# Choosing VectorE's key tiles while the order is planned, instead of from a fixed list, with new pacing constants (attention + MLP on one core)

## The chip, the cores and the metric

The kernel runs on one core of one Trainium2 chip. The metric is device time in microseconds (us). Before the change three runs gave 844.11, 850.04 and 851.01 us, median 850.04. The span is the time from the first to the last instruction of the profiled execution; the granted clock is the share of TensorE's full clock that it was given. TensorE is called PE; the profile calls VectorE DVE, ScalarE ACT and GpSimd POOL.

## The reference, cut to what matters

```python
x = A_x                                    # 1 x 2048 x 512, bf16
xn = layernorm(x)
qkv = (xn @ wqkv)                          # 32 heads of 16
p = softmax(q k^T / 4);  a = (p v) @ wo
h = gelu_tanh(layernorm(x) @ w1 + b1)      # 1792 wide
return x + a + (h @ w2 + b2)
```

With 32 heads of width 16 the costly part is not the products but the exponentials: 32 x 2048 x 2048 of them.

## The kernel before

The work is cut into 32 groups: four heads and 512 queries each. A group has 16 key tiles of 128 keys, and a key tile is four units, one per head. A unit is one 128x512 score matmul into one PSUM bank. Units go one of two ways:

- ScalarE takes units in tiles of two or three PSUM banks and writes `exp` to SBUF.
- VectorE reads the four units of a key tile from PSUM, turning each score by an add and a maximum into the bits of an f16 number (an approximate exponential). It then makes four copies with shifted bits, and PE adds up five weighted products with V, which mends the approximation.

```python
# ScalarE's way (line 1137)
nc.scalar.activation(p_sb[:, s0:s1, :]..., ps[:, b0:b0 + n, :]..., AF.Exp, scale=1.0 / STEP)
# VectorE's way: four reads of PSUM (line 1182), then four shifted copies (line 1205)
nc.vector.tensor_scalar(out=ib[sl][:, j, :], in0=ps[:, pool.bank(key), :],
                        scalar1=LEVEL, scalar2=0.0, op0=ALU.add, op1=ALU.max)
nc.vector.tensor_scalar(out=tb[x % NTB]..., in0=ib[sl]..., scalar1=float(SHIFT[t]),
                        scalar2=None, op0=ALU.add)
```

Nothing is decided on the chip. A planner in the Python code gives every operation a duration and a priority, lists the operations engine by engine, and so fixes the order of the instructions when the kernel is built. For PE it may choose among all candidates that could start within `TOL` of the earliest, and may delay the scores that feed ScalarE by up to `OVER`:

```python
TOL = 0.225
OVER = 0.4
...
end = min(x[0] for x in hot) + self.OVER         # hot: operations that feed ScalarE
cand = [c for c in cand if c[1] in hot or c[0] + c[1].dur + (...) <= end]
...
t, op = min((c for c in cand if c[0] <= first + tol), key=lambda c: (c[1].prio - ..., c[1].seq))
```

How many key tiles of each group VectorE gets stands in a list (111 in all), which fixes ScalarE's stream of tiles before planning starts:

```python
KD = (2, 5, 8, 11, 14)
KD_OF = [(KD if g > 1 else KD2)[:n] for g, n in enumerate((0, 0, 2, 4, 4, 4, 4, 4, 3, ...))]
...
units += [(g, k, j) for g in range(2, NG) for k in range(NT) if k not in KD_OF[g]
          for j in range(HS)]
```

The sums of every group are normalised by a detour: the row sums go by DMA to DRAM and back, are inverted on VectorE, go to DRAM again, and come back spread over 128 partitions (the broadcast, `rlb`). The planner gives the issue of this last DMA 0.5 us and believes that it lands 2.2 us after that, so 2.7 us after the issue begins:

```python
e3 = add("SP", 0.5, lambda: I(nc.sync.dma_start(rlb[:], bcast(rdram[i2]))),
         [e3, last_rlb[0]], pr - 500, lat=2.2)
```

PE also runs matmuls on zeros ("fill"), where the planner expects it to be idle; they are meant to keep its clock up.

## Time and profile before

| | before |
|---|---|
| time, median of 3 | 850.04 us |
| profiled execution | 846.28 us, span 844.5 us, mean granted clock 0.987 |
| ScalarE | 782.0 us busy, 62.5 idle |
| PE | 774.2 us busy, of it 64.2 on fill |
| VectorE | 742.2 us busy |
| ScalarE's waits on scores | 39.8 us in 72 |

How they are read, and the lines themselves, stand in the prediction.

### The profile page before, as it was taken

What the parts mean: (1) busy time and instruction counts of PE and PEld (TensorE: products, weight loads), DVE (VectorE), ACT (ScalarE), POOL (GpSimd) and SP (SyncE); (2) the same over time, 40 slices, a digit from 0 to 9 for tenths busy, and PEclk for the clock granted to TensorE, in tenths of its full rate; (3) what the DMA queues carried; (4) which work ended last, traced back from release to release, by engine and by line L of the source; (5) the groups of instructions that cost most, each with busy time, mean ns of one, the idle gap of its engine ahead of it and who ended that gap; (6) DMA issues with size and microseconds to landing.
All of it is one profiled execution on the core that took longest, in us unless ns stands there. A gap on an engine that the chain in (4) does not pass through costs nothing.

```text
span 844.5 us, 23945 instructions
## 1 busy us (share of the span) xinstructions
PE 774.2 (92%) x10251; PEld 260.6 (31%) x10251; DVE 742.2 (88%) x1281; ACT 782.0 (93%) x681; POOL 55.5 (7%) x163
## 2 busy tenths in 40 slices
PE   6999989999989999998988899999989999998996
PEld 3333333233323332322323233323322333322332
DVE  6867989988999979779899979996699998997987
ACT  3999999999999999999999899998999999998995
POOL 2300000000000000000000000000001000000101
PEclk9999999999999999999999999999999999999998
DMA  5400220000010210000001021000001012101000
GB/s 175 114 2 3 65 59 26 11 15 28 23 31 32 53 37 27 22 21 3 15 22 34 22 52 53 21 14 21 23 16 36 25 28 60 32 10 28 25 10 33
DMA packets 54800, 28.03 MB, mean 33 GB/s; under 512 B 40613, under 2 KB 50598, under 8 KB 54690
## 3 DMA queue, kind: packets, MB, share of 16 engines
q1 hardware_dynamic: 52818, 25.03, 10.8%
q8 instruction: 81, 1.33, 0.7%
q10 hardware_dynamic: 1872, 1.44, 0.6%
q14 instruction: 29, 0.24, 0.1%
HBM read 23.85 MB, written 2.61 MB: 31 GB/s over the span
## 4 chain that ended last, share of the span: by engine, by line
DVE 41%; PE 31%; ACT 12%; issue 8%; DMA 7%; POOL 0%; DVEq 0%; ACTq 0%; SPq 0%
DVE x_sb L1182 16%; ACT p_sb L1137 12%; PE ps L569 12%; DVE tb_x L1205 10%; PE ps L1009 9%; PE ps L991 9%; DMA rlb<-rdram 6%; DVE x_sb L1205 5%; DVE ht L1360 2%; DVE osb L1239 1%; DVE ont L1253 1%; PE ps L1514 1%; DMA rdram<-rc 1%; DVE stats L684 1%; DVE wkv L1393 1%
## 5 line engine op out<-in xcount | busy, mean ns | idle before, releaser
L1137 ACT ACTIVATE p_sb<-ps 128x1024 bf16<-128x1024 f32 (+1 forms) x655 | 741.2, 1247 | 43.7 <-PE ps L991 39.8
L1182 DVE TENSOR_SCALAR x_sb<-ps 128x512 int16<-128x512 f32 x444 | 296.4, 681 | 30.9 <-PE ps L991 30.3
L991 PE MATMUL ps<-qz,kt 32*128 32x512 bf16 x2048 | 280.3, 383 | 39.4 <-ACT p_sb L1137 29.7
L1205 DVE TENSOR_SCALAR tb_x<-x_sb 128x2048 int16<-128x2048 int16 x296 | 198.8, 683 | 2.9 <-PE ps L1009 1.4
L991 PEld LDWEIGHTS <-kt 32*128 32x128 bf16 x2048 | 79.7, 91 | 280.5 <-issue 276.3
L1009 PE MATMUL ps<-p_sb,va 128*32 128x512 bf16 x1604 | 128.6, 386 | 2.4 <-DVE x_sb L1182 2.0
L1009 PE MATMUL ps<-tb_x,vs 128*32 128x512 f16 x1184 | 109.8, 388 | 2.1 <-DVE tb_x L1205 2.0
L1205 DVE TENSOR_SCALAR x_sb<-x_sb 128x2048 int16<-128x2048 int16 x148 | 100.8, 681 | 1.5 <-PE ps L1009 0.7
L1009 PEld LDWEIGHTS <-vs 128*32 128x32 bf16 x1776 | 48.8, 95 | 70.7 <-issue 51.6
L1514 PE MATMUL ps<-ones_bf,zeros_bf 128*32 128x512 bf16 x708 | 64.2, 407 | 4.7 <-issue 3.1
L1009 PEld LDWEIGHTS <-va 128*32 128x32 bf16 x2048 | 40.1, 94 | 83.6 <-issue 79.2
L1009 PE MATMUL ps<-x_sb,vs 128*32 128x512 f16 x592 | 58.9, 386 | 3.9 <-DVE x_sb L1205 3.1
L1260 POOL TENSOR_SCALAR okt<-lc 128x16 f32<-128x16 f32 x31 | 13.7, 442 | 734.3 <-DMA lc<-ldram 734.3
L569 PE MATMUL ps<-yT,w_r 128*32 128x512 bf16 x896 | 58.4, 380 | 3.6 <-DVE x_sb L1182 1.6
L569 PE MATMUL ps<-w_sb,ht 128*32 128x512 bf16 x896 | 60.5, 385 | 0.0
L1009 PE MATMUL ps<-x_sb,va 128*32 128x512 f16 x444 | 44.4, 389 | 3.4 <-DVE osb L1239 2.3
L1360 DVE TENSOR_SCALAR ht<-ps,b_sb 128x512 bf16<-128x512 f32 x56 | 41.7, 744 | 4.8 <-PE ps L569 4.4
L1253 DVE TENSOR_TENSOR ont<-osb,rlb 128x512 bf16<-128x512 f32 x31 | 21.3, 686 | 20.4 <-DMA rlb<-rdram 20.4
L569 PE MATMUL ps<-wo_pad,ont 128*32 128x512 bf16 x512 | 34.6, 384 | 1.1 <-DVE ont L1289 1.1
L569 PEld LDWEIGHTS <-w_r 128*32 128x32 bf16 x896 | 23.5, 96 | 28.1 <-issue 11.7
L569 PEld LDWEIGHTS <-ht 128*32 128x32 bf16 x896 | 21.4, 97 | 24.6 <-issue 9.6
L1514 PEld LDWEIGHTS <-zeros_bf 128*32 128x32 bf16 x708 | 17.2, 99 | 35.7 <-issue 31.7
(92 smaller groups left out, 371.8 us busy)
## 6 DMA issues: line engine op xcount, KB each, us to landing
rlb<-rdram SPq DMA_DIRECT2D x31, 256.0 KB
w_r<-in_B_w_dram SPq DMA_DIRECT2D x56, 128.0 KB
x_r<-in_A_x_dram SPq DMA_DIRECT2D x16, 128.0 KB
w_sb<-in_B_w_dram SPq DMA_DIRECT2D x1, 1792.0 KB
out_dram<-ot SPq DMA_DIRECT2D x12, 128.0 KB
x_sb<-in_A_x_dram SPq DMA_DIRECT2D x2, 512.0 KB
wkv<-in_A_wqkv_dram ACTq DMA_DIRECT2D x1, 512.0 KB
x_sb<-in_A_x_dram ACTq DMA_DIRECT2D x1, 512.0 KB
```

The lines of the kernel that those rows point to most:

```text
L569: I(nc.tensor.matmul(dst[32 * j:32 * j + 32], lhsT=lhsT[:, 32 * j:32 * j + 32], rhs=rhs, start=start, stop=stop, tile_position=(0, 32 * j)))
L684: I(nc.vector.bn_stats(out=stats[:, t, :], in_=x_sb[:, t, :]))
L991: I(nc.tensor.matmul(ps[:, bank, :], lhsT=kt[lo:lo + 32, s // 2, k * P:(k + 1) * P], rhs=qz[lo:lo + 32, (qt * NB + s // 2) % NQB, s % 2, : ...
L1009: I(nc.tensor.matmul(ps[32 * j:32 * j + 32, o_bank[g], :], lhsT=vals[:, h * VS:h * VS + 32], rhs=wts(j), start=st, stop=(pv_left[g] == 0), ...
L1137: I(nc.scalar.activation(p_sb[:, s0:s1, :].rearrange("p a b -> p (a b)"), ps[:, b0:b0 + n, :].rearrange("p a b -> p (a b)"), AF.Exp, scale ...
L1182: I(nc.vector.tensor_scalar(out=ib[sl][:, j, :], in0=ps[:, pool.bank(key), :], scalar1=LEVEL, scalar2=0.0, op0=ALU.add, op1=ALU.max))
L1205: I(nc.vector.tensor_scalar(out=tb[x % NTB].rearrange("p j q -> p (j q)"), in0=ib[sl].rearrange("p j q -> p (j q)"), scalar1=float(SHIFT[t ...
L1239: e0 = add("DVE", dve(QW), lambda: I(nc.vector.tensor_copy(osb[:, i2, :], ps[:, o_bank[g], :])), pvs + before, pr - 1000, rel=(o_done(g),))
L1253: e4 = add("DVE", dve(QW), lambda: I(nc.vector.tensor_tensor(out=ont[:, slot, :], in0=osb[:, i2, :], in1=rlb[:], op=ALU.mult)), [e3] + lis ...
L1260: I(nc.gpsimd.tensor_scalar(out=okt[:, 0, :], in0=lc[:, i2, :], scalar1=L_MIN, scalar2=None, op0=ALU.is_ge))
L1360: I(nc.vector.tensor_scalar(out=ht[:, fc, :], in0=ps[:, misc.bank(key), :], scalar1=b1_sb[:, fc:fc + 1], scalar2=None, op0=ALU.add))
L1514: I(nc.tensor.matmul(ps[32 * j:32 * j + 32, OB if opened is None else o_bank[opened], :], lhsT=zeros_bf[:, 0:32], rhs=ones_bf[:], start=op ...
```

## The change

The intent: let the planner decide which key tiles go to VectorE, at the moment in the plan at which VectorE is nearly through with what it has. The list goes; every group from the third on keeps five spare key tiles, and whichever engine gets there first takes them.

```diff
-    KD_OF = [(KD if g > 1 else KD2)[:n] for g, n in enumerate((0, 0, 2, 4, 4, ...))]
+    left_d = {g: list(KD) if g > 1 else [] for g in range(NG)}
+    left_a = {g: [k for k in range(NT) if k not in KD] if g > 1 else [] for g in range(NG)}
...
+    def next_d():
+        if len(todo) >= OPEN or d_busy[0] >= OUT:          # OPEN 1, OUT 3
+            return
+        g0 = max(stream["g"], 2)
+        for g in (g0, g0 + 1):                             # this group or the next
+            if g >= NG or not left_d[g]:
+                continue
+            if g == stream["g"] and units_left(g) + HS * len(left_d[g]) < (RES if g < NG - 1 else RESL):
+                continue
+            k = left_d[g][0]
+            deps = qk_deps(g, k)
+            if deps is None or not all(o.done for o in deps):   # its K and Q must be projected
+                return
...
+            left_d[g].pop(0)
+            todo.append((g, k, [0, 1, 2, 3]))
+            d_busy[0] += 1
+            build_dve(g, k)
+            return
...
+            k = left_a[g].pop(0) if left_a[g] else left_d[g].pop()    # ScalarE takes what is left
```

With it comes a new set of constants (cut):

```diff
-    TOL = 0.225
+    TOL = 0.075
-    OVER = 0.4
+    OVER = 0.3
-    OUT0, OUT1 = 0.775, 0.4
-    HLO, HHI, DN0, DN1 = 0.09, 0.42, 0.5, 0.12
-    PAIR = 2
-    VX = 0
-    HOT = 4
+    OUT0, OUT1 = 0.475, 0.25
+    HLO, HHI, DN0, DN1 = 0.09, 0.36, 0.5, 0.12
+    PAIR = 1
+    VX = 1
+    KTP, QTP = 70.0, 70.0
+    HOT = 1
-    RATE, QO, PO, AO, DO = 24.25, 55.0, 47.0, 35.0, 32.0
+    RATE, QO, PO, AO, DO = 23.75, 55.0, 39.5, 25.0, 17.0
-            pr = T0 + KG * tq - 4 if b == 0 else ts_(2 * b, tq / 4.0) - 40
+            pr = T0 + KG * tq - 4 if b == 0 else ts_(2 * b, tq / 4.0) - KTP      # projection of K
-        pr = ts_(2 * n) - 50.0
+        pr = ts_(2 * n) - QTP                                                    # projection of Q
```

The `KTP` and `QTP` edits make the projections of K and Q due 70 us ahead of their group, instead of 40 and 50. At the very start, transposes, projections and fill are one 128-column matmul (`mm1`) where four 32-column ones stood.

## The prediction

> **What bounds the kernel now.** I read the page's engine shares first, then its groups, then who ScalarE waited for, then single stretches in order of time.
>
> ```profile
> span 844.5 us, 23945 instructions
> ...
> PE 774.2 (92%) x10251; PEld 260.6 (31%) x10251; DVE 742.2 (88%) x1281; ACT 782.0 (93%) x681; POOL 55.5 (7%) x163
> ...
> L1137 ACT ACTIVATE p_sb<-ps 128x1024 bf16<-128x1024 f32 (+1 forms) x655 | 741.2, 1247 | 43.7 <-PE ps L991 39.8
> L1182 DVE TENSOR_SCALAR x_sb<-ps 128x512 int16<-128x512 f32 x444 | 296.4, 681 | 30.9 <-PE ps L991 30.3
> L1205 DVE TENSOR_SCALAR tb_x<-x_sb 128x2048 int16<-128x2048 int16 x296 | 198.8, 683 | 2.9 <-PE ps L1009 1.4
> L1514 PE MATMUL ps<-ones_bf,zeros_bf 128*32 128x512 bf16 x708 | 64.2, 407 | 4.7 <-issue 3.1
> ```
>
> Three engines are nearly full at once. The work is 32 groups (four heads, 512 queries) of 16 key tiles; a key tile is four units, each the scores of one head for 128 keys. A key tile goes either to ScalarE (Exp, L1137) or to VectorE (four PSUM reads at L1182, then four shifted copies at L1205). 444 instructions at L1182 are 111 key tiles on VectorE; the other 401 are on ScalarE. ScalarE is the fullest: 782.0 of 844.5 us, so 62.5 us idle. That idle time is all a better order can win. Of it, 14.9 us lie in the first 42.2 us (27.3 busy there; the first Exp starts at 16.9) and about 9 after the last Exp ends at 834.0. Neither end is touched much. Some 38 us in the middle are left, and ScalarE's own list of waits gives nearly all of it to score matmuls (L991). PE is 92% busy, but L1514 is warm-up work on zeros, 177 sets of four matmuls, so it is not the bound by volume. It is the bound by order: when does it get to the next scores? The worst kind looks like this in the timeline:
>
> ```profile
> 484.52 1.38 PE L569 MATMUL ps<-wo_pad,ont 128*32 128x512 bf16 x16
> ...
> 485.84 0.61 PE L991 MATMUL ps<-qz,kt 32*128 32x512 bf16 x6
> ...
> 486.34 1.45 ACT L1137 ACTIVATE p_sb<-ps 128x1536 bf16<-128x1536 f32 x1 [1.88 <-PE ps L991]
> ```
>
> PE ran other products since the last scores, and ScalarE waited 1.88 us for them. I went through every gap of ScalarE over 0.15 us between 30 and 833 us: 71 gaps, 36.9 us. In each I counted the sets of four 32-column matmuls ("quads") that PE ran between the awaited scores and the scores before: 44 gaps (23.5 us) follow six quads or more, 8 (2.65 us) five, 10 (3.6 us) four or fewer, and in 9 (7.2 us) PE itself sat waiting, mostly for VectorE. The windows show a second thing:
>
> ```profile
> 567.50:570.00 2.50, 2.50 (x18) 0.60 (x18) 2.42 (x5) 2.48 (x2) 1.11 (x4) 0.50 0.02 2
> 570.00:572.50 2.50, 2.50 (x28) 0.94 (x24) 1.20 (x3) 2.49 (x3) 0.00 (x0) 0.50 0.07 10
> ```
>
> The figure before the last two is the granted TensorE clock. Four stretches, about 17 us together (from some 165, 482, 567 and 765 us), ran at 0.50. Three of the 44 gaps (1.19, 1.88 and 2.75 us, together 5.8) follow them at once.
>
> **What the Trainium skill says.** "TensorEngine Tiling (Array Packing)", Key Properties: changing the tiling mode drains TensorE. The kernel alternates between 32-row scores and 32-column products, so each alternation should cost something. The chain agrees:
>
> ```profile
> 27.47 0.86 PE ps L569 x16
> 28.33 0.32 PE ps L991 x2
> 28.66 0.98 PE ps L569 x16
> ```
>
> Four quads take 0.86 us after products of their own mode (0.215 each) and 0.98 after scores: 0.12 us for the change. "TensorE: Matmul & The Clock Gate", The HAM clock gate: the array falls to half clock after about an idle window of 3.4 us, and the window runs free of the program. The 0.50 entries agree in height and length; with a free-running window their number can differ between executions, which would fit three runs of 844.11, 850.04 and 851.01 us (not shown). "ScalarE: Activation LUTs", What ACT_TABLE_LOAD costs: 0.833 ns per element, and back-to-back activations overlap by about 93 ns. In the trace the two large forms add up to 437.3 + 373.6 us while their group covers 741.2, an overlap of 107 ns each. So a key tile costs ScalarE 741.2/401 = 1.85 us. "VectorE: DVE Perf Modes", The perf-mode tier table: 693 ns for a 2048-element 16-bit scalar operation; here 683. Eight of them cost a VectorE key tile 8 x 0.68 = 5.4 us alone, or 4.8 where they follow without a gap (two take 1.20 us in the chain).
>
> **The change part by part.** Everything is still fixed when the kernel is built. Before, a list said how many key tiles of each group VectorE gets; the rest was cut into ScalarE tiles in a fixed sequence. Now the planner gives VectorE its next key tile when fewer than three are open, never in the first two groups, and only while ScalarE keeps enough units. With it come new pacing constants: PE picks among candidates within 0.075 us, not 0.225, may delay the scores that feed ScalarE by 0.3, not 0.4, and products with V are issued per key tile, not in pairs. I compared the built programs' instruction order, which gives counts and no times:
>
> 1. Division: 111 VectorE key tiles become 110; groups 2 to 31 still get 3 to 5 each (before 2 to 5). ScalarE gains four units: 4 x 741.2/1604 = **+1.8 us** on the fullest engine. VectorE loses 5.4 us, which ends nothing.
> 2. Score alternation: mode changes go from 1178 to 1338. 160 x 0.12 = 19 us more on PE. Beside them, fill matmuls fall from 177 quads to 79 (17 of these now one 128-column matmul): 98 x 0.215 = 21 us less. Another 16 quads go (3 us), because the first transposes and projections are 128 columns wide. PE's sum is about 5 us lower: no gain by itself.
> 3. Stretches between scores, the part I count on: of six quads or more 82 become 25; of five, 36 become 79; shorter ones 469 become 563. At the old cost per stretch: outside the half-clock stretches, 17.7 us over 79 long stretches is 0.224 each, so 25 cost 5.6: **-12.1**. Five quads: 2.65/36 = 0.074, times 79 = 5.8: **+3.2**. Short: 3.6/469, times 563 = 4.3: **+0.7**. The 7.2 us in which PE waited and the 5.8 us at half clock stay.
>
> Sum: 1.8 - 12.1 + 3.2 + 0.7 = -6.4 us. That is cautious, as it assumes that the new order places its short stretches as carelessly as the old one. If the narrower tolerances put five quads only where ScalarE works on a three-unit tile (1.48 us, longer than 5 x 0.215 + 0.12), the short and five-quad gaps vanish and 36.9 becomes 5.6 + 7.2 + 5.8 = 18.6: -18.3 + 1.8 = -16.5 us. The middle is -11.5; I take -12. The diff's own target pace points to the upper end: 24.25 to 23.75 us per group over 30 groups is -15 us, but a target is no measurement.
>
> **The rivals.** (a) *The division was never the limit and the new order only moves the waits.* For it: the division is nearly the same, PE remains about as full, the DMA round trip behind VectorE stays (the waits list 20.4 us of VectorE waiting for rlb). PE at 92% cannot serve everybody at once: if scores go first, products with V come later, the 15 slots of p_sb fill, and ScalarE waits for those. In the old trace ScalarE waited for L1009 only once (1.1 us), so slots are not short now. It would give 843 to 850 us. (b) *VectorE becomes the bound*, as it takes key tiles greedily and delays the evictions that PE needs. Against it: 742.2 us before, fewer tiles after. It would appear as more than 7.2 us of PE waiting for VectorE; worth up to +5 us. (c) *Half clock*: with 98 fewer fill quads, PE could drop below the activity that keeps its clock. Each of the old stretches of 3.4 us cost ScalarE roughly 1.2 to 2.9 us; four more would eat 8 us. Against it: the fills vanished because the order leaves less room for them. (d) *Nearly all of the 38 us goes*: the time would be near 818 us; I see no reason why the waits on the DMA and the half clock should go too.
>
> **Range and chances.** The three runs before average 848.4 us; less 12 is **836 us**. A run of before already varies by 7 us, and my sum by 5 either way; rivals (a) and (c) reach up to 848, a gain of 27 us down to 822. So 822 to 848. Faster by over 2% needs about -17 us, the upper end of my sum and a little beyond the target pace: 0.36. Within 2%: 0.60. Slower by over 2% would need a new wait of 29 us net, which nothing in the counts suggests: 0.04.
>
> **What would show it.** ScalarE's busy time stays near 784 us and its wait on scores falls from 39.8 to about 25 us, by fewer waits (72 before), with most of the loss in those after six quads or more. VectorE falls to about 737 us. PE's fill group falls to about a third of 64.2 us. Wrong would be: as many waits of ScalarE as before (rival a, above all if they name products with V), PE waiting for VectorE by more than some 15 us (b), more than four stretches at a clock of 0.50 (c), or a gain made at the head or the tail, where I expect less than 1 us.

## The result, and the profile after

The changed kernel took 822.46, 824.16, 828.22 and 827.35 us, median **825.75**; the kernel before, in the same rounds, 847.9 (four runs). The ratio is 0.9738, 95% interval 0.9677 to 0.9799: faster by 2.6%. Here and below a ratio is the mean time of one kernel's fast runs over the mean of the other's of the same rounds, so it is not quite the ratio of the medians quoted. The profiled execution of the changed kernel is its fastest (822.46), that of before lies between its own (846.28).

The page of the changed kernel, shares first and then the groups of ScalarE, PE's scores and VectorE:

```profile
span 820.5 us, 22781 instructions
...
PE 774.9 (94%) x9671; PEld 256.7 (31%) x9672; DVE 736.4 (90%) x1273; ACT 782.4 (95%) x682; POOL 54.8 (7%) x163
...
L1197 ACT ACTIVATE p_sb<-ps 128x1024 bf16<-128x1024 f32 (+1 forms) x656 | 741.6, 1245 | 17.4 <-PE ps L1032 11.5
L1032 PE MATMUL ps<-qz,kt 32*128 32x512 bf16 x2048 | 316.4, 382 | 27.7 <-DVE x_sb L1274 10.5
L1274 DVE TENSOR_SCALAR x_sb<-ps 128x512 int16<-128x512 f32 x440 | 291.6, 683 | 15.4 <-PE ps L1032 14.1
L1299 DVE TENSOR_SCALAR tb_x<-x_sb 128x2048 int16<-128x2048 int16 x293 | 197.0, 684 | 3.5 <-PE ps L1050 2.5
```

All three engines did nearly the same work (PE 774.2 and 774.9, ScalarE 782.0 and 782.4, VectorE 742.2 and 736.4 us), in 24.0 us less. What went is idle time: ScalarE's fell from 62.5 to 38.1 us. The list of waits (engine, line, what it waited for: total us, times, longest) says for what, first before, then after:

```profile
ACT p_sb L1137 <- PE ps L991: 39.8, 72, 4.0
...
DVE ont L1253 <- DMA rlb<-rdram: 20.4, 13, 2.8
```

```profile
ACT p_sb L1197 <- PE ps L1032: 11.5, 30, 1.5
...
DVE ont L1347 <- DMA rlb<-rdram: 8.4, 10, 2.2
```

ScalarE's wait on scores fell by 28.3 us, and its longest from 4.0 to 1.5 us. What this looks like on ScalarE, in the timeline of one stretch (start, us, what, x how many in a row; in brackets the idle time before it and who ended it), before:

```profile
475.71 4.62 ACT L1137 ACTIVATE p_sb<-ps 128x1536 bf16<-128x1536 f32 x4 [0.36 <-PE ps L991]
481.94 2.52 ACT L1137 ACTIVATE p_sb<-ps 128x1536 bf16<-128x1536 f32 x2 [1.60 <-PE ps L991]
486.34 15.93 ACT L1137 ACTIVATE p_sb<-ps 128x1536 bf16<-128x1536 f32 x14 [1.88 <-PE ps L991]
502.76 11.40 ACT L1137 ACTIVATE p_sb<-ps 128x1536 bf16<-128x1536 f32 x10 [0.49 <-PE ps L991]
```

and after:

```profile
466.77 45.06 ACT L1197 ACTIVATE p_sb<-ps 128x1024 bf16<-128x1024 f32 x39 [0.27 <-PE ps L1032]
512.59 17.64 ACT L1197 ACTIVATE p_sb<-ps 128x1536 bf16<-128x1536 f32 x15 [0.76 <-PE ps L1032]
```

Thirty-nine tiles follow one another without a gap that the view shows, where before the row broke every few tiles.

Where on the time axis did 24.0 us go? The first Exp starts at 14.8 instead of 16.9 us (-2.1), the last ends 25.1 us earlier, so the stretch between them is 23.0 us shorter, and the tail after it is about 1 us longer. I listed ScalarE's gaps over 0.15 us between 30 us and the last Exp as the prediction did, with how many sets of four matmuls ("quads") PE ran between the awaited scores and the scores before:

| PE ran, before the awaited scores | before: gaps, us | after: gaps, us | the prediction's first sum for after |
|---|---|---|---|
| six quads or more, at full clock | 41, 17.7 | 7, 2.3 | 5.6 |
| the same at half clock | 3, 5.8 | 0, 0 | 5.8 (stays) |
| five quads | 8, 2.65 | 7, 3.1 | 5.8 |
| four or fewer | 10, 3.6 | 9, 4.2 | 4.3 |
| PE itself waited | 9, 7.2 | 6, 1.8 | 7.2 (stays) |
| sum | 36.9 | 11.4 | 28.7 |

The half-clock stretches inside the attention part are gone from this execution. The windows (length, busy time with counts of PE, weight loads, VectorE, ScalarE and GpSimd, then granted clock, DMA share, GB/s) show one at the start (and there is one in the tail, where PE has nothing left to do, in both kernels); around 565 us, where before fell to 0.50, it is 1.00:

```profile
10.00:12.50 2.50, 2.50 (x28) 2.45 (x27) 1.03 (x2) 1.25 (x3) 0.00 (x0) 0.60 1.10 340
...
565.00:567.50 2.50, 2.50 (x35) 0.64 (x31) 2.34 (x4) 2.50 (x3) 0.00 (x0) 1.00 0.00 0
```

That is partly luck of the execution. From each run's record, the time at half clock is 2 x (1 - clock) x span. Over the 96 executions of the kernel before in the experiments, it averages 21 us (5 to 39), and a straight line through time against it has a slope of 0.26 us per us (0.27 in the first fit, which the expectations quote; correlation 0.86) and 842.5 us at zero. That is how the two go together, not a cause that was tested. The four runs of the changed kernel average 15 us. At this slope it explains about 2 us of the mean gain of 22; and it explains most of the 844 to 854 us between which the kernel before varies.

### The profile page after: what moved, and what is told of

The parts are those of the page before. It is cut to its first block, busy times and chain, and to the rows that moved or that the text cites. A ratio compares the mean times of both kernels' runs of the same rounds, so it can differ in the third digit from the quotient of the medians.

```text
span 820.5 us, 22781 instructions
## 1 busy us (share of the span) xinstructions
PE 774.9 (94%) x9671; PEld 256.7 (31%) x9672; DVE 736.4 (90%) x1273; ACT 782.4 (95%) x682; POOL 54.8 (7%) x163
## 3 DMA queue, kind: packets, MB, share of 16 engines
q1 hardware_dynamic: 52818, 25.03, 11.2%
## 4 chain that ended last, share of the span: by engine, by line
PE 38%; DVE 33%; ACT 15%; issue 8%; DMA 6%; POOL 0%; SPq 0%; DVEq 0%; ACTq 0%
ACT p_sb L1197 14%; PE ps L597 14%; DVE x_sb L1274 13%; PE ps L1050 12%; PE ps L1032 11%; DVE tb_x L1299 7%; DVE x_sb L1299 4%; DMA rlb<-rdram 4%; DVE ht L1454 2%; DMA rdram<-rc 1%; DVE stats L719 1%; DVE osb L1333 1%; DVE ont L1347 1%; DVE vs L923 1%; DMA ldram<-osb 1%
## 5 line engine op out<-in xcount | busy, mean ns | idle before, releaser
L1197 ACT ACTIVATE p_sb<-ps 128x1024 bf16<-128x1024 f32 (+1 forms) x656 | 741.6, 1245 | 17.4 <-PE ps L1032 11.5
L1032 PE MATMUL ps<-qz,kt 32*128 32x512 bf16 x2048 | 316.4, 382 | 27.7 <-DVE x_sb L1274 10.5
L1274 DVE TENSOR_SCALAR x_sb<-ps 128x512 int16<-128x512 f32 x440 | 291.6, 683 | 15.4 <-PE ps L1032 14.1
L1032 PEld LDWEIGHTS <-kt 32*128 32x128 bf16 x2048 | 85.5, 91 | 281.1 <-issue 275.0
L1050 PE MATMUL ps<-p_sb,va 128*32 128x512 bf16 x1608 | 158.6, 389 | 0.2 <-DVE x_sb L1274 0.2
L1050 PEld LDWEIGHTS <-va 128*32 128x32 bf16 x2048 | 48.2, 93 | 109.0 <-issue 106.8
L597 PEld LDWEIGHTS <-w_r 128*32 128x32 bf16 x896 | 21.6, 96 | 25.3 <-issue 12.1
L1333 DVE COPY osb<-ps 128x512 f32<-128x512 f32 x31 | 21.2, 683 | 8.4 <-PE ps L1050 8.4
L1464 ACT ACTIVATE ht<-ht 128x3584 bf16<-128x3584 bf16 x8 | 25.1, 3182 | 0.0
```

The lines of the kernel that those rows point to most:

```text
L597: I(nc.tensor.matmul(dst[32 * j:32 * j + 32], lhsT=lhsT[:, 32 * j:32 * j + 32], rhs=rhs, start=start, stop=stop, tile_position=(0, 32 * j)))
L1032: I(nc.tensor.matmul(ps[:, bank, :], lhsT=kt[lo:lo + 32, s // 2, k * P:(k + 1) * P], rhs=qz[lo:lo + 32, (qt * NB + s // 2) % NQB, s % 2, : ...
L1050: I(nc.tensor.matmul(ps[32 * j:32 * j + 32, o_bank[g], :], lhsT=vals[:, h * VS:h * VS + 32], rhs=wts(j), start=pv_done[g] == 1, stop=end, ...
L1197: I(nc.scalar.activation(p_sb[:, s0:s1, :].rearrange("p a b -> p (a b)"), ps[:, b0:b0 + n, :].rearrange("p a b -> p (a b)"), AF.Exp, scale ...
L1274: I(nc.vector.tensor_scalar(out=ib[sl][:, j, :], in0=ps[:, pool.bank(key), :], scalar1=LEVEL, scalar2=0.0, op0=ALU.add, op1=ALU.max))
L1333: e0 = add("DVE", dve(QW), lambda: I(nc.vector.tensor_copy(osb[:, i2, :], ps[:, o_bank[g], :])), pvs + before, pr - 1000, rel=(o_done(g),))
```

## The experiments

The change has four separable parts: the division it arrives at, the constants, the wide matmuls at the start, and the sharing while planning. The theories before the runs: **Theory 1**, the sharing itself does it, as the planner has a free hand over both streams. **Theory 2**, the division of the key tiles. **Theory 3**, the constants alone, above all the narrow tolerances. After the first four runs came **Theory 4**: the sharing pays, but only with the longer lead of the K and Q projections. Twelve kernels ran, all correct.

### The new division in the old kernel

```diff
-... enumerate((0, 0, 2, 4, 4, 4, 4, 4, 3, 3, 3, 5, ...
+... enumerate((0, 0, 4, 3, 3, 3, 4, 3, 4, 4, 4, 3, ...      # the counts the changed kernel arrives at
```

> The kernel before, with only its list of VectorE key tiles per group replaced by the numbers that the changed kernel arrives at (110 in all). Theory 1 (the gain is the order in which PE reaches the scores; the division hardly matters): long stretches between scores stay at 79 (82 before), so 843 to 852 us, ratio 0.995 to 1.005. Theory 2 (the better division is the gain): most of the 22 us, 826 to 832 us.

Measured: 851.83 us (20 runs) against 847.84 for before; ratio 1.0035 (1.0015 to 1.0056). Theory 2 falls.

### The new constants in the old kernel

```diff
-    TOL = 0.225
+    TOL = 0.075          # and all the other constants above, the lead of 70 included
```

> The kernel before, fixed division kept, with every pacing constant that both kernels share set to its new value. Theory 3 (the retuned constants alone carry the gain): 826 to 832 us. Theory 1: the constants need the sharing that is decided while planning; long stretches fall only to 56 and stretches of five quads rise to 91, so by the cost per stretch of the kernel before -5 and +4 us: 842 to 856 us.

Measured: 865.3 us (4 runs), ratio 1.0206 (1.0155 to 1.0258). ScalarE's waits on scores grew from 39.8 us in 72 to

```profile
ACT p_sb L1137 <- PE ps L991: 49.6, 89, 4.6
```

The constants alone make the old kernel slower, more than any theory allowed. Theory 3 falls.

### The old constants in the new kernel

```diff
-    TOL = 0.075
+    TOL = 0.225
...
-    KTP, QTP = 70.0, 70.0
+    KTP, QTP = 40.0, 50.0          # and all the other constants back
```

> The changed kernel with the shared pacing constants set back to their old values (107 key tiles on VectorE). Theory 1: the sharing keeps more than half of the gain, 828 to 838 us (49 long stretches instead of 25, three key tiles more on ScalarE: +5.5 us). Theory 3: back to 843 us or more.

Measured: 848.86 us (12 runs), ratio 1.0001 (0.998 to 1.0021): no gain at all, where Theory 1 wanted 828 to 838. So neither half of the change gains anything alone. The timeline of this run shows where it loses:

```profile
146.68 0.62 PE L1032 MATMUL ps<-qz,kt 32*128 32x512 bf16 x7 [3.98 <-DVE kt L885]
...
147.38 2.37 ACT L1197 ACTIVATE p_sb<-ps 128x1024 bf16<-128x1024 f32 x2 [8.83 <-PE ps L1032]
```

ScalarE stands for 8.83 us, and the scores that release it waited for `kt`, a piece of K just projected. A second such wait of 5.43 us follows at 156.83. In the kernel before, the list of waits has none of PE for a piece of K or Q. This gave Theory 4.

### The wide matmuls of the start in the old kernel

```diff
-                    mm(ps[:, bk, jc * P:(jc + 1) * P], ...
+                    (mm if t > 3 else mm1)(ps[:, bk, jc * P:(jc + 1) * P], ...
```

and likewise for the first projections and the fill before the start.

> The kernel before with only the matmuls of its start made 128 columns wide (first transposes, first projections, warm-up); the order is otherwise the same. If the earlier start of the first Exp (14.8 instead of 16.9 us in the two profiles) comes from these: first Exp near 14.8 us and about 2 us off the time, ratio 0.9975. If it comes from something else, or is absorbed later: first Exp near 16.9, ratio 1.000.

Measured: 852.88 us (15 runs), ratio 1.0061 (1.0043 to 1.008): slower, though the start did get shorter. The timeline of before has, ahead of the first scores,

```profile
15.91 0.60 PE L1514 MATMUL ps<-ones_bf,zeros_bf 128*32 128x512 bf16 x5 [3.08 <-issue]
```

3.08 us in which PE waited for nothing that the profile shows, after some 220 small matmuls. With a quarter of the instructions this is 0.22 us, and the first Exp starts at 15.05 instead of 16.88:

```profile
13.95 0.74 PE L1518 MATMUL ps<-ones_bf,zeros_bf 128*128 128x512 bf16 x2 [0.22 <-issue]
...
15.05 2.85 ACT L1141 ACTIVATE p_sb<-ps 128x1024 bf16<-128x1024 f32 x3 [0.81 <-PE ps L995]
```

The rest of the order is the same as before, yet the 1.8 us are lost again by 101 us, where VectorE waits for the broadcast, PE for VectorE, and ScalarE for PE:

```profile
98.34 0.69 DVE L1257 TENSOR_TENSOR ont<-osb,rlb 128x512 bf16<-128x512 f32 x1 [1.75 <-DMA rlb<-rdram]
99.75 1.05 PE L569 MATMUL ps<-yT,w_r 128*32 128x512 bf16 x16 [1.72 <-DVE ht L1364]
101.23 2.37 ACT L1141 ACTIVATE p_sb<-ps 128x1536 bf16<-128x1536 f32 x2 [2.26 <-PE ps L995]
```

This broadcast was issued at 92.91 us, and at 91.43 in the kernel before, so it comes 1.5 us later although the start was earlier. All waits on the broadcast add up to 27.9 us (before 20.4). So a head start alone is worth nothing here. That accounts for the gain being lost, not for the 5 us on top: its runs had 28 us at half clock on average against 21, which is about 2 us by the slope above. The rest stays open, and so does the cause of the 3.08 us: the trace has in that pause the first 16 KB transfer of the instruction queue (from 13.28 us, 1.16 us long), which with the wide matmuls comes only at 17.15 us; that PE waited for it is not shown.

### The short lead in the new kernel

```diff
-    KTP, QTP = 70.0, 70.0
+    KTP, QTP = 40.0, 50.0
```

> The changed kernel with one pair of constants back: the K and Q projections are planned 40 and 50 us ahead of their group, as before, not 70. Theory 4 (sharing while planning can only take a key tile whose K and Q are ready, so it needs that lead): the two long waits of the third experiment (8.8 and 5.4 us) come back in large part, 833 to 845 us. Rival (all constants matter a little): 826 to 832 us.

Measured: 847.91 us (20 runs, of which one, at 854.33, is slow and left out of the ratio), ratio 0.9999 (0.998 to 1.0018). This one line takes the whole gain away, more than Theory 4 had allowed. The timeline of its longest wait:

```profile
723.99 1.04 PE L597 MATMUL ps<-xnT,wq_sb 128*32 128x512 bf16 x16
...
726.21 0.37 PE L1032 MATMUL ps<-qz,kt 32*128 32x512 bf16 x1 [1.19 <-DVE qz L908]
...
727.37 2.37 ACT L1197 ACTIVATE p_sb<-ps 128x1024 bf16<-128x1024 f32 x2 [6.85 <-PE ps L1032]
```

The projection of Q that the next scores need comes at 723.99. From 717 us on PE had run chains of the MLP's first product instead, which share one slot for sums in PSUM with the projections, one chain at a time; the projection stood in line behind them. ScalarE stopped for 6.85 us. Four more waits of this kind, all behind a piece of K, are 4.64, 3.41, 2.81 and 2.45 us long, between 129 and 154 us. Together the five are 20.2 us, and the gaps of this run are 31.9 us against 11.4: the missing lead is nearly all of the difference. Its runs also had about 31 us at half clock against 15, some 4 us by the slope above; whether the stops bring the half clock was not tested.

### The long lead in the old kernel

```diff
-            pr = T0 + KG * tq - 4 if b == 0 else ts_(2 * b, tq / 4.0) - 40
+            pr = T0 + KG * tq - 4 if b == 0 else ts_(2 * b, tq / 4.0) - 70.0
-        pr = ts_(2 * n) - 50.0
+        pr = ts_(2 * n) - 70.0
```

> The kernel before with only the lead of the K and Q projections at 70 us. If the lead is a gain by itself: 832 to 840 us. If it only pays together with the sharing (Theory 4: the fixed division never starved for K or Q, its waits name no K or Q eviction): no gain, 846 to 858 us (92 stretches of six quads or more, 82 before).

Measured: 850.69 us (20 runs), ratio 1.0028 (1.0012 to 1.0044). The old kernel has no use for the lead, having no such waits. With this there are both leads for each way of planning:

| ratio to before | lead 40/50 | lead 70/70 |
|---|---|---|
| fixed list | 1 | 1.0028 |
| shared while planning, other new constants | 0.9999 | 0.9738 |
| shared while planning, old constants (next section for the right one) | 1.0001 | 0.9853 |

The first and the last row differ in the sharing (and the wide matmuls at the start, which alone gain nothing), not in the constants.

### The old constants but the long lead, in the new kernel

```diff
 # of the changed kernel, everything but KTP, QTP back to the old constants
-    TOL = 0.075
+    TOL = 0.225
...
```

> The third experiment (changed kernel, old constants) with only the lead at its new 70 us. Theory 4: its two long waits (14.3 us) go, 832 to 838 us, so the sharing without the other constants gains about 12 us. Rival (tolerances, pairs and the other constants carry it; 45 stretches of six quads or more instead of 25): 843 us or more.

Measured: 835.08 us (4 runs), ratio 0.9853 (0.9813 to 0.9893). The lead is the only difference to the run at 848.86, so it is worth 14 us with the old constants too. The other new constants, which hurt the old kernel, bring the remaining 9 us here (835.08 to 825.75; the runs with the old constants had 35 us at half clock against 15, some 5 of the 9 by the slope above). In the built order this kernel has 45 stretches of six quads or more between scores; the changed one has 25.

### Only one key tile open on VectorE

```diff
-    OUT, OPEN, ... = 3, 1, ...
+    OUT, OPEN, ... = 1, 1, ...
```

> The changed kernel, but VectorE may have one key tile open instead of three, so it takes the next only when the last shifted copy of the one before is in the plan. 91 key tiles instead of 110 reach VectorE. If the looking ahead is what keeps VectorE supplied: ScalarE gains 19 x 1.85 = 35 us of work, VectorE loses about 100, 845 to 862 us. If it does not matter because PE is the limit: under 833 us.

Measured: 860.17 us (4 runs), ratio 1.0152 (1.0105 to 1.02). The page shows why:

```profile
PE 791.5 (92%) x9703; PEld 264.6 (31%) x9704; DVE 663.2 (77%) x1121; ACT 812.2 (95%) x713; POOL 56.1 (7%) x163
```

VectorE gets 91 key tiles instead of 110 and idles; ScalarE takes the rest and is 29.8 us busier. Looking up to three tiles ahead is part of what makes sharing work: "nearly through" must not mean "idle".

### More fill in the old kernel

```diff
-    NEED = 9.5
+    NEED = 99.0          # 221 more fill quads
```

> The kernel before with fill matmuls in every planned pause of PE (398 quads instead of 177). If half clock costs what the runs of the kernel before say (0.27 us for each us at half clock, 21 us of it on average, so 5.6 us) and fill prevents it: clock 0.996 or more and 842 to 845 us. If the fills mostly delay the scores, or half clock costs nothing: 848 us or more.

Measured: 848.36 us (12 runs), ratio 1.0006 (0.9989 to 1.0022). The time at half clock did fall, from 20 to 14 us, worth about 2 us at the slope above, but the time did not; the expectation of 842 to 845 us for fill that pays missed, and the other one, 848 or more, came true. That the extra fill stands in the way of other work by as much as it saves is likely but was not traced. So more clock alone brings no gain either.

### The real duration of the broadcast in the plan

In the chain of waits of the kernel before, the broadcast of 256 KB stands ten times, with 4.58 to 5.46 us from the start of its issue to its landing, such as

```profile
117.99 5.46 DMA rlb<-rdram
```

while the plan has 2.7 (0.5 for the issue, 2.2 after it). The Trainium skill's "DMA: Bandwidth & Descriptors", Anatomy of one DMA, gives a fit of 2.0 us plus bytes/436e3 for the GpSimd path, an estimate of 2.6 us for this size. This transfer is issued by SyncE and repeats each row for 32 partitions; the measurement decides.

```diff
-                 [e3, last_rlb[0]], pr - 500, lat=2.2)
+                 [e3, last_rlb[0]], pr - 500, lat=4.8)
```

> The changed kernel with one planned duration corrected: the broadcast of the row sums' reciprocals is planned at 4.8 us, as measured, not 2.2. If VectorE's 8.4 us of waiting for it still cost ScalarE something: VectorE's wait for it under 3 us and 818 to 823 us. If those waits are hidden: 824 to 829 us.

Measured: 819.35 us (4 runs), ratio 0.9661 (0.9613 to 0.971), against 0.9738 (0.9677 to 0.9799) for the changed kernel. VectorE's wait for the broadcast fell from 8.4 to 0.7 us, and ScalarE's on scores from 11.5 to 8.8:

```profile
ACT p_sb L1197 <- PE ps L1032: 8.8, 28, 1.1
...
DVE ont L1347 <- DMA rlb<-rdram: 0.7, 1, 0.7
```

ScalarE's gaps fell from 11.4 to 8.5 us. These four runs had only 4 us at half clock, against 15, so some 3 of the 6 us are the clock's. The other 3 agree with the gaps, but another order alone can shift the time by as much.

### Constants tuned anew, with and without the real duration

```diff
-    TOL = 0.075
+    TOL = 0.0942
-    ..., DN0, DN1 = ..., 0.5, 0.12
+    ..., DN0, DN1 = ..., 0.5394, 0.1161
-    F2 = 400.0
+    F2 = 316.614
-    HOLD = 25.0
+    HOLD = 18.791
-    RATE, QO, PO, AO, DO = 23.75, 55.0, 39.5, 25.0, 17.0
+    RATE, QO, PO, AO, DO = 23.75, 67.4378, 39.5, 25.0, 19.6818
-                 [e3, last_rlb[0]], pr - 500, lat=2.2)
+                 [e3, last_rlb[0]], pr - 500, lat=4.8)
```

> The changed kernel with that duration corrected and seven constants chosen again for it; long stretches 20 instead of 25, of five quads 57 instead of 79. If the order of PE and the DMA duration are what is left: 814 to 821 us. If what is left of the gaps is half clock and the two ends: 823 us or more.

Measured: **812.97 us** (4 runs, 809.58 to 816.72), ratio 0.9563 (0.9513 to 0.9613). It beats both kernels: 4.4% under before, and 12.8 us under the changed kernel's median.

The control is a kernel with its constants tuned in the same way (RATE 23.87, QO 65.1, SLK 50.3, RES 22 and a few more), but the duration left at 2.2:

```diff
-    OUT, OPEN, RES, RESL, SLK, ALP = 3, 1, 20, 24, 40.0, 25.0
+    OUT, OPEN, RES, RESL, SLK, ALP = 3, 1, 22, 24, 50.2612, 25.0
-    RATE, QO, PO, AO, DO = 23.75, 55.0, 39.5, 25.0, 17.0
+    RATE, QO, PO, AO, DO = 23.87, 65.0994, 39.5, 25.0, 17.0
...
```

> The changed kernel with eleven constants chosen again but the broadcast still planned at 2.2 us; long stretches 15, of five quads 62. If the wrong DMA duration in the plan hurts, this is slower than the run before it by 2 us or more although its stretches are as short; if not, equal: 814 to 821 us.

Measured: 827.16 us (4 runs), ratio 0.973 (0.9675 to 0.9784): nothing gained. Its order has only 15 stretches of six quads or more (the changed kernel 25, the best 20), so by the prediction's way of counting it should be the best of the three. Its list of waits says otherwise:

```profile
ACT p_sb L1197 <- PE ps L1032: 26.4, 41, 3.2
...
DVE ont L1347 <- DMA rlb<-rdram: 14.5, 10, 2.8
```

An order that is polished against a wrong duration meets the real one on the chip: VectorE stands 14.5 us for the broadcast. That ScalarE's 26.4 us on scores come from it was not traced wait by wait. What is shown is that the two tuned kernels differ by 14 us, in the duration and in their constants (some 2 us by half clock, 23 us against 17). The control is not a clean one: eleven constants were chosen anew here and seven there, and those seven with the duration left at 2.2 did not run.

## Why the prediction was right, and where it was off

The predicted 836 us with a range of 822 to 848 holds the measured 825.75, but at its lower end, and "within 2%", its likeliest class, did not come true: the gain was 22 us where 12 were foreseen.

*What bounds it.* Right. The three engines' busy times stood still and ScalarE's idle time made the whole difference.

*Division (point 1).* Right: ScalarE's busy time rose by 0.4 us (foreseen 1.8), VectorE fell by 5.8, and the division alone gains nothing in the old kernel.

*Alternation and fill (point 2).* Right as to counts and in that it is no gain by itself, but not in size. The fill group fell from 64.2 to 28.0 us (22.5 and 5.5 in its two forms), so by 36 us where 21 were foreseen, and PE's busy time still rose by 0.7 us where the sum had about 5 less: the rest of PE's records grew by 37 us, not by 16. How much of that is drain at a change of mode was not measured.

*Stretches between scores (point 3).* The mechanism was right and its terms mis-sized, as the table of gaps shows. The first sum had 28.7 us for after; 11.4 were measured, 17.3 less. Of these 17.3, the long stretches are 3.3 (cost 0.33 each when they end in a gap, but 7 of 25 did) and those of five quads 2.7. The larger part, 11.2 us, is in the sentence "The 7.2 us in which PE waited and the 5.8 us at half clock stay". They did not: PE's own waits cost 1.8 us, and in the profiled execution no half-clock stretch hit the attention part. Holding a term constant because the change does not name it was the step that failed. For the half clock the mean over runs shows about 2 us, so most of those 5.8 us belong to the profiled execution and not to the change.

*The head.* "Less than 1 us" was wrong for the head: the first Exp starts 2.1 us earlier (with the longer tail, both ends together gained about 1 us). The 3.08 us without a visible cause were in the trace of before, and I had not asked what removes them. The run with the head alone shows that such a start can be lost again.

*What it did not weigh.* The lead of the projections stood in the diff and in none of the sums. The short-lead run shows that without it the sum would have been a promise the kernel could not keep: the shared streams reach for K and Q sooner than the MLP's queue lets them be made. That the prediction came near the truth with this half of the cause unseen was luck: it took for granted that no new wait would come, and the lead, which it did not weigh, made that so. Its counts hardly see the lead. Counted in the traces, the short-lead order has 41 stretches of six quads or more where the changed kernel has 25, worth 4 us at its 0.224 each, and the lead is worth 22.

*Half clock.* The prediction takes from the skill that half clock follows an idle window of 3.4 us, and finds the entries to agree in height and length. They do (0.50, and 3.4 us or twice that), but the cause does not: in the 3.4 us before the four stretches begin, PE's longest waits were 0.23, 1.89, 0.50 and 1.63 us. So half clock came here after waits far shorter than 3.4 us.

*Rivals.* (a), that waits only move: no, though the new kernel with a short lead is just that case. (b), VectorE as the bound: PE's scores waited 10.5 us for VectorE's reads, but in pieces of at most 0.6 us, and the gaps in which PE itself waited were only 1.8 us. The sign named for (b), over 15 us of PE waiting for VectorE, tells nothing: all such waits in the list add up to 26 us before and 25 after. (c), more half clock: the reverse. (d), nearly all of the 38 us: 25.5 of 36.9 went; I gave it too little, for the reason "I see no reason why the waits on the DMA and the half clock should go too". The waits on the DMA fell from 20.4 to 8.4 us, and with a true duration in the plan to 0.7.

Four things stay open: what PE waited for in the 3.08 us of the head, the 5 us by which the head alone makes the old kernel slower, the size of the loss with the constants alone, and the share of each single constant. Every edit gives a wholly different order, and two orders differ by several us for no reason that one could name in advance; the runs above separate only the effects larger than that.

## What to carry to other kernels

Two streams that share work freely can reach for something that the old fixed order had always made in time, as these did for K and Q; look for what the shared items depend on, and make that early enough in the same change. When a term of a sum "stays", ask what holds it there. And when a plan orders the instructions, compare its durations with the trace first: here one DMA was planned at 2.7 us and took about 5. Correcting it came with 6 us, of which the slope gives some 3 to the clock; a choice of eleven new constants without it came with none.

## What the Trainium skill lacked or had wrong

- "TensorE: Matmul & The Clock Gate", The HAM clock gate: the page's figures for the cost of half clock (under Terms, half of the throttled time, as an estimate for K/N at 4/8; further on, a ramp of under 1% of a span) are not for a kernel in which ScalarE is the fullest engine. Here each us at half clock went with 0.26 us of time over 96 executions, and 5 to 39 us of it with times from 844 to 854. The page has half clock come "after ≥1 idle window (~3.4µs)" and no figure for how much activity is enough: in the kernel before, a stretch at 0.50 begins at the end of the window below (mean clock 0.93), in which PE was busy for 2.00 of 2.50 us, with no wait in it longer than 0.50 us:

```profile
565.00:567.50 2.50, 2.00 (x22) 0.53 (x18) 2.50 (x6) 2.50 (x2) 0.00 (x0) 0.93 0.07 23
```

- "TensorEngine Tiling (Array Packing)", Key Properties: the drain at a change of mode has no figure. In the chain of the kernel before, four quads took 0.12 us more after scores than after products of their own mode (0.98 and 0.86).
- "DMA: Bandwidth & Descriptors", Anatomy of one DMA: the fit, an estimate of 2.6 us for 256 KB, is for another issuing engine and is too low for this broadcast from DRAM to 128 partitions issued by SyncE, which took 4.58 to 5.46 us from the start of its issue. What the page says elsewhere of how a transfer is spread over the DMA engines was not tried on it, so this is not shown to be a gap of the page.
- No page was found with a figure for the stall at the start: 3.08 us under "issue" after some 220 small matmuls with weight loads, and 0.22 us where a quarter of the instructions did the same work. The pages on how instructions are fetched were not tried on it.
